# Attention products on 64x64 quarters, natural channel order, and moved q rows in a fused attention and feed-forward kernel

## The chip, the cores and the metric

The kernel runs on one core of a Trainium2 chip. A core has TensorE (PE, matrix products into PSUM), VectorE (DVE), ScalarE (ACT), GpSimd (POOL) and SyncE (SP); SP, POOL and ACT also start DMAs. The metric is the device time of one execution in microseconds (us). A profile of one execution gives every instruction's start and duration. On TensorE, "PEld" are the loads of the stationary operand and "PE" the matmuls, which are pipelined: a matmul's own duration is longer than the distance to the next one.

## What is computed

```python
q_s = exp(q - max(q, -1));  q_s /= sum(q_s, -1)        # softmax over the 64 channels of a head
k_s = exp(k - max(k, 2));   k_s /= sum(k_s, 2)         # softmax over the 576 rows of a head
kv  = einsum('bhsd,bhse->bhde', k_s, v)                # 64 x 64 for each head
x   = einsum('bhsd,bhde->bhse', q_s, kv)               # 576 x 64 for each head
x   = x.transpose(0, 2, 1, 3).reshape(4608, 512)       # row b*576+s, channel h*64+e
h   = x @ w_in                                         # 512 -> 2048
out = maximum(0.01 * h, h) @ w_out                     # 2048 -> 512
```

There are 8 batches, 8 heads, 576 rows and 64 channels a head, all in float32; the kernel multiplies in bfloat16.

## The kernel before

**Attention of one batch.** q, k and v lie in SBUF with 128 partitions: a partition holds nine rows of one head (`r`, 0 to 8), and one tile holds the eight heads as four pairs. A head's 576 rows are thus 64 partitions (`l`) by nine `r`. "Row r" below means these 64 rows of every head. Heads are counted as h = 4 gg + 2 hp + hh: hh is the upper or lower half of the partitions, gg and hp choose the pair. For k there are a maximum (`k_tree`, `k_allmax`), a subtraction (`k_sub`) and an exponential on ACT (`k_exp`); v is cast to bfloat16 with a column of ones beside it (`v_cast`). `kv_quads` (L318) multiplies exp(k) by v with 64x64 quarters of the array, 72 matmuls of 65 columns a batch, the last column being k's sum. `kd_make` (L338), or `kd_rec` and `kd_one` (L403, L407) in batch 0, divide by that sum and write `kd`: for each of four channel blocks g = 2 hh + gg a 128 x 128 matrix with the two heads hp = 0, 1 on its diagonal and zeros elsewhere (set once by POOL). q has a maximum (`q_max`), a subtraction on POOL (`q_sub`), an exponential on ACT (`q_exp`), a sum and reciprocal (`q_sum`) and a multiplication (`q_norm`) on VectorE, and a transpose. Batches 0 and 1 are transposed by TensorE (`q_transpose`) and copied out of PSUM (`q_keep`); later batches by a DMA that SP starts (`q_turn`). `attend` (L441) and `attend_x` (L468) then multiply `kd` by the transposed q, one full 128 x 128 matmul for each channel block and group of rows, and copy each product from PSUM into `xT`, which holds x transposed: 128 channels by 4608 rows in four blocks. Its channel blocks are in the order g = 2 hh + gg, so `load_w_in` (L130) permutes w_in's rows to match.

**Feed-forward.** The 4608 rows are nine tiles of 512. Layer 1 has 16 blocks j of 128 hidden channels, each four matmuls (channel blocks cb) into one PSUM bank, then `leaky` on ACT into `gj`. Layer 2 has four row blocks of 128 rows, 16 matmuls each, and VectorE copies the result out (`store`); SP writes it to memory. PSUM's eight banks are six of pool psB (layer 1, attention) and two of psO (layer 2).

**Order.** Every engine executes its instructions in the order of the code. `at(t, u, ...)` hangs attention work behind place u of tile t. In tiles 1 to 8 places 0 to 15 are the j of layer 1, and places 16 to 31 come after every four matmuls of layer 2 (19, 23, 27 and 31 end its row blocks); a place of 32 or more is one of the next tile. In tile 0 places 0 to 31 are the j of layer 1, first for rows 0 to 255 of the tile and then for rows 256 to 511, and 32 to 47 the j of layer 2, where all four row blocks take part in each j. Batch b is worked on in tiles b - 2 and b - 1 (`plan`), batch 2 in tile 1 (`plan2`), batches 0 and 1 ahead of and in tile 0. A batch has 576 rows and a tile 512, so tile 1 ends after row 6 of batch 1 and tile 2 after row 5 of batch 2.

**Loads.** SP loads q, k, v of batch 0, POOL starts w_in in eight pieces (four for hidden channels 0 to 1023, four for the rest). `hold_sync(0, ...)` (L599) makes SP wait for the first piece of the second half before it loads batch 1. POOL reads an element of the whole w_in (L607) before it starts five of w_out's six pieces. `hold_sync(1, ...)` (L610) makes SP wait for the piece of w_out with j = 8 to 11 before batch 2.

**Front of tile 0.** `begin` and `end` split layer 1's first half: blocks j = 0, 2, 4, 6 (two j a bank) take the channel blocks as products become ready, then j = 8 to 14, with pieces of batch 0's attention (x1, x3, t1, t2, x2) between.

Of the kernel before, what the change touches and what calls it, by code (L numbers as in the profile page):

```python
# [20 lines left out]
R = 9  # L21
# [4 lines left out]
def kernel(  # L26
# [99 lines left out]
    w_in_r = moe_w_in.rearrange("(gg hp hh d) f -> gg hp d hh f", gg=2, hp=2, hh=2)  # L126

    w_in_t = w_in_sb.rearrange("p (hh gg) f -> p gg hh f", gg=2)

    def load_w_in(fh):  # L130
        fs = slice(fh * (F // 2), (fh + 1) * (F // 2))
        for gg in range(2):
            for hp in range(2):
                nc.gpsimd.dma_start(  # L134
                    out=w_in_t[hp * D : (hp + 1) * D, gg, :, fs], in_=w_in_r[gg, hp, :, :, fs]
                )
# [201 lines left out]
    def kd_make(b):  # L338
        for hh in range(2):
            pkv = st[b]["pkv"][hh]  # L340
            krec = small_pool.tile([P, 2, 1], FP32, name="krec")
            nc.vector.reciprocal(out=krec, in_=pkv[:, :, D : D + 1])
            for hp in range(2):
                p0 = hp * D
                nc.vector.tensor_tensor(  # L345
                    out=kd2[b % 2][p0 : p0 + D, 2 * hh : 2 * hh + 2, p0 : p0 + D],
                    in0=pkv[p0 : p0 + D, :, 0:D],
                    in1=krec[p0 : p0 + D].to_broadcast([D, 2, D]),
                    op=ALU.mult,
                )  # L350

    wake_ps = psO_pool.tile([P, TT], FP32, name="pout")
# [54 lines left out]
    def kd_one(eng, b, gg, hh):  # L407
        pkv, krec = st[b]["pkv", gg][hh], st[b]["krec", gg, hh]
        eng.scalar_tensor_tensor(
            out=kd2[b % 2][:, 2 * hh + gg].rearrange("p (h d) -> p h d", h=2),  # L410
            in0=pkv[:, 0:D].unsqueeze(1).to_broadcast([P, 2, D]),
            scalar=krec,
            in1=block.rearrange("p (h d) -> p h d", h=2),
            op0=ALU.mult,
            op1=ALU.mult,
        )

    def q_transpose(b, r0, n):
        ps = psB_pool.tile([P, NB, n, L], BF16, name="psum_qt", tag=BANK_TAG)
# [21 lines left out]
    def attend(b, gs, c0, n, eng):  # L441

        ps = psB_pool.tile([P, len(gs), n], FP32, name="po", tag=BANK_TAG)
        for i, g in enumerate(gs):
            nc.tensor.matmul(
                ps[:, i],
                lhsT=kd2[b % 2][:, g],
                rhs=st[b]["qT"][:, g].rearrange("c r l -> c (r l)")[:, c0 : c0 + n],
                start=True,
                stop=True,  # L450
            )
        step = gs[-1] - gs[0] if len(gs) == 2 else 1
        o = xT[:, gs[0] : gs[-1] + 1 : step, b * S + c0 : b * S + c0 + n]
# [4 lines left out]


# [8 lines left out]
    def attend_x(b, g, rs, eng):  # L468
        hh, gg = divmod(g, 2)
        n = (rs.stop - rs.start) * L  # L470
        ps = psB_pool.tile([P, n], FP32, name="po", tag=BANK_TAG)
        qX = st[b]["qX"].rearrange("c (r g) (h l) -> c g h r l", g=2, h=2)
        nc.tensor.matmul(  # L473
            ps.rearrange("p (r l) -> p r l", l=L), lhsT=kd2[b % 2][:, g], rhs=qX[:, gg, hh, rs]
        )
        c0 = b * S + rs.start * L
        o = xT[:, g, c0 : c0 + n]
        if eng is nc.scalar:
            eng.copy(out=o, in_=ps)  # L479
        else:  # L480
            eng.tensor_copy(out=o, in_=ps)

    def layer1(j, ph, c0, n, part=slice(0, 4), first=True, last=True):
        for i, cb in list(enumerate((0, 2, 1, 3)))[part]:
# [4 lines left out]
                start=(i == 0 and first),  # L489
                stop=(i == NB - 1 and last),  # L490
# [36 lines left out]
    GS = (0, 2, 1, 3)  # L527
# [56 lines left out]
    attend(0, [0], 0, 256, nc.scalar)  # L584
    attend(0, [2], 0, 256, nc.scalar)
# [18 lines left out]
    def behind_first_units():  # L604
# [34 lines left out]
    def plan(b, o):  # L639
# [9 lines left out]
        kvu, pu = o + (24 if b == 3 else 25), o + (33 if b == 3 else 34)  # L649
# [3 lines left out]
        for i in range(8):  # L653
            at(t, pu + i // 2, lambda i=i: attend_x(b, i // 2, XR[i % 2], nc.scalar))


    def plan2():
# [13 lines left out]
        for i in range(8):  # L671
            at(1, 28 + i // 2, lambda i=i: attend_x(b, GS[i % 4], XR[i // 4], nc.scalar))
# [42 lines left out]
    for j, ph in zip(J0, begin(J0, ((0, x1), (1, x3)))):  # L715
        end(j, ph, 0, slice(2, 4), False)
# [72 lines left out]
```

## Time and profile before

| | us |
|---|---|
| median of 3 runs (lowest, highest) | 288.9 (288.86, 289.06) |
| the profiled execution: its time, its span | 288.9, 287.1 |
| before layer 1 of tile 0 | 0 to 15.0 |
| tile 0, layer 1 | 15.0 to 33.85 |
| tile 0, layer 2 | 33.85 to 51.38 |
| tiles 1, 2 | 29.52, 29.58 |
| tiles 3 to 6 | 29.45, 29.44, 29.42, 29.42 |
| tile 7 (no attention left) | 27.63 |
| tile 8 and the last stores | 31.26 |

Rows of a timeline give the start, the busy time, the engine, the line (L) of the kernel, the operation, output<-input, the shape and the number of instructions; in brackets stands the idle time before them and what ended it. TensorE's clock was granted in full (1.00) in all of these stretches.

### The profile page before, as it was taken

How to read it: one execution, taken by the hardware profiler on the slowest of the kernel's cores; microseconds unless marked ns; L12 is line 12 of the kernel's file. 1: busy time of each engine (PE TensorE's matmuls, PEld its weight loads, DVE VectorE, ACT ScalarE, POOL GpSimd, SP SyncE). 2: the span in 40 equal slices, each digit the busy share in tenths (PEclk: the TensorE clock that was granted, in tenths of full speed). 3: DMA queues.
4: the chain of work that ended last, by engine and by line, in shares of the span. 5: the costliest groups of instructions: out<-in, count | busy, mean ns of one | idle time of the engine just before them, and what ended most of it. 6: DMA issues, size and time to landing. Idle time of an engine off the chain costs nothing.

```text
span 287.1 us, 4854 instructions
## 1 busy us (share of the span) xinstructions
PE 275.8 (96%) x1927; PEld 136.4 (48%) x1954; DVE 145.7 (51%) x247; ACT 149.4 (52%) x272; POOL 89.6 (31%) x66
## 2 busy tenths in 40 slices
PE   8778999999999999999999999999999999999995
PEld 3357745444544444444444444444445444444443
DVE  3976946996880895398185727663631100110011
ACT  4965874567269407932774358434953065016400
POOL 4965550017049009604900590049100000000000
PEclk9999999999999999999999999999999999999999
DMA  7999999686659264963398239913131310130032
GB/s 257 317 210 354 288 181 404 170 274 258 134 109 378 106 142 104 398 159 82 76 379 195 56 82 351 237 37 80 32 84 37 73 37 3 45 81 20 2 73 73
DMA packets 36598, 45.79 MB, mean 159 GB/s; under 512 B 15968, under 2 KB 19296, under 8 KB 36576
## 3 DMA queue, kind: packets, MB, share of 16 engines
q1 hardware_dynamic: 33120, 41.16, 48.2%
q0 software_dynamic: 3296, 4.20, 8.3%
q8 instruction: 15, 0.25, 0.3%
q10 hardware_dynamic: 160, 0.13, 0.1%
q14 instruction: 7, 0.06, 0.1%
HBM read 36.70 MB, written 9.44 MB: 161 GB/s over the span
## 4 chain that ended last, share of the span: by engine, by line
PE 82%; DMA 10%; DVE 2%; POOL 1%; issue 1%; SPq 1%; ACT 1%; DVEq 0%; ACTq 0%
PE pout L506 39%; PE ph L485 38%; DMA v_raw<-in_v_dram 5%; DMA w_in_sb<-in_moe_w_in_dram 3%; PE po L473 2%; DMA k_raw<-in_k_dram 2%; PE pkv L323 2%; DVE qe L310 1%; DVE qsum L303 1%; SPq L79 1%; POOL w_in_sb L134 1%; POOL vb L216 0%; ACT qe L294 0%; PE psum_qt L422 0%; SPq L538 0%
## 5 line engine op out<-in xcount | busy, mean ns | idle before, releaser
L506 PE MATMUL pout<-w_out_sb,gj 128*128 128x512 bf16 (+2 forms) x580 | 129.5, 373 | 0.6
L485 PE MATMUL ph<-xT,w_in_sb 128*128 128x512 bf16 (+1 forms) x626 | 127.0, 357 | 3.0 <-DMA w_in_sb<-in_moe_w_in_dram 1.7
L494 ACT ACTIVATE gj<-ph 128x512 bf16<-128x512 f32 x144 | 81.8, 603 | 54.6 <-PE ph L485 54.0
L485 PEld LDWEIGHTS <-w_in_sb 128*128 128x128 bf16 x640 | 62.0, 98 | 64.1 <-issue 3.5
L506 PEld LDWEIGHTS <-gj 128*128 128x128 bf16 x592 | 56.8, 98 | 62.1 <-ACT gj L494 0.4
L500 DVE COPY out_sb<-pout 128x512 f32<-128x512 f32 (+1 forms) x34 | 22.7, 676 | 85.7 <-PE pout L506 80.0
L196 POOL TENSOR_TENSOR k_raw<-k_raw,kall 128x2304 f32<-128x2304 f32 (+1 forms) x6 | 29.1, 4856 | 80.1 <-DVE kall L188 67.5
L286 POOL TENSOR_TENSOR q_raw<-q_raw,qmax 128x2304 f32<-128x2304 f32 (+4 forms) x12 | 31.3, 2618 | 24.1 <-DVE qmax L227 23.7
L303 DVE TENSOR_REDUCE qsum<-qe 128x36 f32<-128x2304 bf16 (+4 forms) x12 | 19.9, 1661 | 36.4 <-ACT qe L294 36.4
L479 ACT CAST xT<-po 128x320 bf16<-128x320 f32 (+1 forms) x48 | 16.8, 402 | 40.0 <-PE po L473 40.0
L204 ACT ACTIVATE ke<-k_raw 128x2304 bf16<-128x2304 f32 (+2 forms) x11 | 17.6, 1597 | 10.5 <-POOL k_raw L196 9.0
L310 DVE TENSOR_TENSOR qe<-qe,qrec 128x2304 bf16<-128x2304 bf16 (+4 forms) x11 | 19.9, 1809 | 0.3
L227 DVE TENSOR_REDUCE qmax<-q_raw 128x36 f32<-128x2304 f32 (+4 forms) x12 | 19.6, 1649 | 0.0
L294 ACT ACTIVATE qe<-q_raw 128x2304 bf16<-128x2304 f32 (+4 forms) x12 | 17.0, 1420 | 0.0
L216 POOL CAST vb<-v_raw 128x1152 bf16<-128x1152 f32 x13 | 14.6, 1151 | 0.0
L163 DVE TENSOR_TENSOR t<-k_raw 128x1024 f32<-128x1024 f32 (+1 forms) x10 | 10.1, 1012 | 0.9 <-DMA k_raw<-in_k_dram 0.5
L163 DVE TENSOR_TENSOR t<-t 128x256 f32<-128x256 f32 (+2 forms) x20 | 9.6, 478 | 0.7
L473 PE MATMUL po<-qX,kd 128*128 128x320 bf16 (+1 forms) x48 | 9.8, 286 | 0.0
L500 ACT COPY out_sb<-pout 128x512 f32<-128x512 f32 (+1 forms) x3 | 1.7, 563 | 14.9 <-PE pout L506 14.9
L356 PE MATMUL pout<-zero 128*128 128x512 bf16 x23 | 7.5, 462 | 1.4 <-POOL zero L101 1.3
L345 DVE TENSOR_TENSOR kd<-pkv,krec 64x128 bf16<-64x128 f32 x28 | 8.1, 288 | 0.7
L323 PEld LDWEIGHTS <-ke 64*64 64x64 bf16 x576 | 5.6, 106 | 3.7 <-ACT gj L494 1.7
(62 smaller groups left out, 104.7 us busy)
## 6 DMA issues: line engine op xcount, KB each, us to landing
out_dram<-out_sb SPq DMA_DIRECT2D x70, 128.0 KB, 2.4
q_raw<-in_q_dram SPq DMA_DIRECT2D x7, 1152.0 KB, 8.0
v_raw<-in_v_dram SPq DMA_DIRECT2D x7, 1152.0 KB, 11.2
k_raw<-in_k_dram SPq DMA_DIRECT2D x6, 1152.0 KB, 5.5
k_raw<-in_k_dram SPq DMA_DIRECT2D x4, 576.0 KB, 5.5
w_in_sb<-in_moe_w_in_dram POOLq DMA_DIRECT2D x8, 256.0 KB, 7.5
v_raw<-in_v_dram SPq DMA_DIRECT2D x2, 576.0 KB, 7.1
w_out_sb<-in_moe_w_out_dram POOLq DMA_DIRECT2D x4, 256.0 KB, 9.7
```

The costliest lines, as they stand in the source:

```text
L163: nc.vector.tensor_tensor(out=o, in0=i0, in1=i1, op=ALU.max)
L196: eng.tensor_tensor(out=ks, in0=ks, in1=st[b]["kall"][:, hs].unsqueeze(2).to_broadcast([P, n, R, D]), op=ALU.subtract,)
L204: nc.scalar.activation(out=st[b]["ke"][:, :, hs].rearrange("p r h d -> p h r d"), in_=st[b]["k"][:, hs], func=AF.Exp,)
L227: nc.vector.tensor_reduce(out=m, in_=st[b]["q"][:, :, rs], axis=AX.X, op=ALU.max)
L286: eng.tensor_tensor(out=qs, in0=qs, in1=st[b]["qmax", rs.start].unsqueeze(3).to_broadcast([P, HL, n, D]), op=ALU.subtract,)
L294: nc.scalar.activation(out=st[b]["qe"][:, rs].rearrange("p r h d -> p h r d"), in_=st[b]["q"][:, :, rs], func=AF.Exp,)
L303: nc.vector.reduce_sum(out=qsum, in_=st[b]["qe"][:, rs], axis=AX.X)
L310: eng.tensor_tensor(out=qes, in0=qes, in1=st[b]["qrec", rs.start].unsqueeze(3).to_broadcast([P, n, HL, D]), op=ALU.mult,)
L485: nc.tensor.matmul(ph, lhsT=w_in_sb[:, cb, j * P : (j + 1) * P], rhs=xT[:, cb, c0 : c0 + n], start=(i == 0 and first), stop=(i == NB - 1 a ...
L494: nc.scalar.activation(out=o, in_=ph, func=AF.Prelu, alpha=LEAKY_SLOPE)
L500: copy(out=out_sb, in_=pout)
L506: nc.tensor.matmul(pout, lhsT=g_sb[j // 2][:, j % 2, tsub * P : (tsub + 1) * P], rhs=w_out_sb[:, j, os], start=(j == 0), stop=(j == NF - 1),)
```

## The change

- `kd` holds for each head its 64 x 64 matrix alone, without zeros. `cross` multiplies it by that head's transposed q on one 64x64 quarter: rows of the quarter by hp, columns by hh, so four heads (one gg) go to four quarters, with the outputs of hp = 0 and hp = 1 in two banks. Channel blocks of `xT` are then 2 gg + hp, the natural order of channels, and w_in is loaded in natural order, one piece for each channel block and half.
- A batch's products stand at one place of the code (`attend_all`): all quarters first, then the copies out of PSUM. For batches 3 to 7 that is place 27 (b < 5) or 23 of tile b - 1, for rows 0 to 7 and row 8; before, they stood in four pairs at four places between 19 and 31. Batch 2: rows 0 to 5 at place 27 of tile 1, rows 6 to 8 at place 19 of tile 2.
- Batch 1: rows 0 to 6 in tile 0. Rows 7 and 8 (RE): maximum at place 31, subtraction and exponential at 32 and 44 of tile 0, sum and norm at place 12 of tile 1, transposes at 15, products at 23. One of v's two casts goes from ACT to POOL, and the exponential of rows 0 to 3 moves ahead of the other cast.
- Batch 0: the front of tile 0 is rewritten. Each group of blocks takes cb 0, 1, 2 in `begin` and cb 3 in `end_pe`; `leaky` comes in `end_act`. The second half no longer starts between the pieces of the first. The norm of rows 4 and 5 goes from POOL to VectorE, two transposes use psO.

```diff
-    block = const_pool.tile([P, P], FP32)
-    nc.gpsimd.memset(block, 0.0)
-    for p0 in range(0, P, D):
-        nc.gpsimd.memset(block[p0 : p0 + D, p0 : p0 + D], 1.0)
...
-    kd2 = [const_pool.tile([P, NB, P], BF16, name=f"kd{i}") for i in range(2)]
+    kd2 = [const_pool.tile([P, 2, 2, D], BF16, name=f"kd{i}") for i in range(2)]
...
-        nc.gpsimd.memset(kd2[i], 0.0)
...
+        for cb in range(NB):
+            nc.gpsimd.dma_start(out=w_in_sb[:, cb, fs], in_=w_in_r[:, cb, fs])
...
-            for hp in range(2):
-                p0 = hp * D
-                nc.vector.tensor_tensor(
-                    out=kd2[b % 2][p0 : p0 + D, 2 * hh : 2 * hh + 2, p0 : p0 + D],
...
+            nc.vector.tensor_tensor(
+                out=kd2[b % 2][:, :, hh],
+                in0=pkv[:, :, 0:D],
+                in1=krec.to_broadcast([P, 2, D]),
+                op=ALU.mult,
+            )
...
+        eng.tensor_tensor(
+            out=kd2[b % 2][:, gg, hh], in0=pkv[:, 0:D], in1=krec.to_broadcast([P, D]), op=ALU.mult
+        )
...
+    def cross(b, gg, outs, rows):
+        for hp in range(2):
+            for hh in range(2):
+                half = slice(hp * D, (hp + 1) * D)
+                if "qX" in st[b]:
+                    rhs = st[b]["qX"].rearrange("c (r g) (h l) -> c g h r l", g=2, h=2)[:, gg, hh, rows]
+                else:
+                    rhs = st[b]["qT"][:, 2 * hh + gg, rows]
+                nc.tensor.matmul(
+                    outs[hp][hh * D : (hh + 1) * D].rearrange("p (r l) -> p r l", l=L),
+                    lhsT=kd2[b % 2][half, gg, hh],
+                    rhs=rhs[half],
+                    start=True,
+                    stop=True,
+                )
+
+    def attend(b, ggs, rows):
+        n = (rows.stop - rows.start) * L
+        ps = [
+            psB_pool.tile([P, len(ggs), n], FP32, name="po", tag=BANK_TAG) for _ in range(2)
+        ]
+        for i, gg in enumerate(ggs):
+            cross(b, gg, [ps[hp][:, i] for hp in range(2)], rows)
+        st[b]["po", ggs, rows.start] = ps
+
+    def x_keep(eng, b, ggs, rows, hp):
+        ps = st[b]["po", ggs, rows.start][hp]
...
+        o = xT[:, s0 : 2 * ggs[-1] + hp + 1 : 2, c0:c1]
...
+    def attend_rows(b, rows, engs=(nc.scalar, nc.scalar)):
+        groups = ((0, 1),) if rows.stop - rows.start <= 4 else ((0,), (1,))
+        for ggs in groups:
+            attend(b, ggs, rows)
+        return [
+            lambda ggs=ggs, hp=hp: x_keep(engs[hp], b, ggs, rows, hp) for ggs in groups for hp in range(2)
+        ]
+
+    def attend_all(b, *parts):
+        for fn in sum([attend_rows(b, *p) for p in parts], []):
+            fn()
...
-    at(0, 0, lambda: q_sum(0, R1), lambda: q_norm(0, R1, nc.gpsimd), behind_first_units)
-    at(0, 2, lambda: q_exp(0, R2), lambda: q_sum(0, R2), lambda: q_norm(0, R2))
...
-    at(0, 26, lambda: attend(0, [0, 1, 2, 3], 512, 64, nc.scalar))
+    at(0, 26, lambda: attend_all(0, (R3, (nc.scalar, nc.vector))))
...
+    RM, RE = slice(4, 7), slice(7, R)
+    for rs in (RA, RM):
+        at(0, 20, lambda rs=rs: q_max(1, rs), lambda rs=rs: q_sub(nc.gpsimd, 1, rs))
+    at(0, 31, lambda: k_exp(1, H1), lambda: k_exp(1, H0), lambda: q_max(1, RE))
...
-    at(0, 32, lambda: v_cast(nc.scalar, 1, 1), lambda: q_exp(1, RB), lambda: q_sum(1, RB))
-    at(0, 41, lambda: kv(1))
-    at(0, 41, lambda: q_norm(1, RB), lambda: kd_make(1))
+    at(0, 32, lambda: v_cast(nc.scalar, 1, 0), lambda: v_cast(nc.gpsimd, 1, 1))
+    at(0, 32, lambda: q_exp(1, RM), lambda: q_sum(1, RM), lambda: q_norm(1, RM))
+    at(0, 32, lambda: q_sub(nc.gpsimd, 1, RE))
     for r0 in (0, 2):
...
+        at(0, 42, lambda r0=r0: q_transpose(1, r0, 2), lambda r0=r0: q_keep(nc.scalar, 1, r0, 2))
+    at(0, 42, lambda: kv(1), lambda: kd_make(1))
+    at(0, 44, lambda: q_transpose(1, 4, 3), lambda: q_keep(nc.scalar, 1, 4, 3), lambda: q_exp(1, RE))
+    at(0, 46, lambda: attend_all(1, (slice(0, 7), (nc.scalar, nc.vector))))
+    at(1, 12, lambda: q_sum(1, RE), lambda: q_norm(1, RE))
+    at(1, 15, lambda: q_transpose(1, 7, 2), lambda: q_keep(nc.scalar, 1, 7, 2))
+    at(1, 23, lambda: attend_all(1, (RE,)))
+
+    XR = (slice(0, 6), slice(6, R))
...
-        for i in range(8):
-            at(t, pu + i // 2, lambda i=i: attend_x(b, i // 2, XR[i % 2], nc.scalar))
+        at(b - 1, 27 if b < 5 else 23, lambda: attend_all(b, (slice(0, 8),), (slice(8, R),)))
...
+        at(1, 27, lambda: attend_all(b, (XR[0],)))
+        at(2, 19, lambda: attend_all(b, (XR[1],)))
...
+    def end_act(j, ph, half):
+        leaky(g_sb[j // 2][:, :, 256 * half : 256 * half + 256], ph)
+        for h in range(2):
             run(0, 16 * half + j + h)
 
-    t1 = (lambda: q_transpose(0, 4, 2), lambda: q_keep(nc.scalar, 0, 4, 2), lambda: q_exp(0, R3))
-    t2 = (lambda: q_transpose(0, 6, 2), lambda: q_keep(nc.vector, 0, 6, 2), lambda: q_sum(0, R3))
+    t2 = (
+        lambda: q_transpose(0, 6, 2, psO_pool, "pout"),
+        lambda: q_keep(nc.vector, 0, 6, 2),
+        lambda: q_sum(0, R3),
+    )
     x2 = (
-        lambda: attend(0, [0, 2], 256, 256, nc.scalar),
-        lambda: attend(0, [1, 3], 256, 256, nc.vector),
+        lambda: attend_all(0, (slice(4, 8), (nc.scalar, nc.vector))),
         lambda: q_norm(0, R3),
     )
-    x1 = (lambda: attend(0, [1], 0, 256, nc.scalar),)
-    x3 = (lambda: q_exp(0, R1), lambda: attend(0, [3], 0, 256, nc.scalar))
-
-    def whole(j):
-        end(j, psB_pool.tile([P, 2, 256], FP32, name="ph", tag=BANK_TAG), 1, slice(0, 4), True)
+    x1 = (
+        lambda: attend(0, (1,), RA),
+        lambda: x_keep(nc.scalar, 0, (1,), RA, 0),
+        lambda: q_exp(0, R1),
+        lambda: x_keep(nc.scalar, 0, (1,), RA, 1),
+    )
 
...
+    begun = list(zip(J0, begin(J0, ((0, x1), (1, ()), (2, ())))))
+    for j, ph in begun:
+        end_pe(j, ph, 0, slice(3, 4), False)
+    for i, (j, ph) in enumerate(begun):
+        end_act(j, ph, 0)
+        if i == 0:
+            q_sum(0, R1)
+            q_norm(0, R1)
+            q_exp(0, R2)
+            late_loads()
+            q_sum(0, R2)
+            q_norm(0, R2)
+        if i == 1:
+            q_transpose(0, 4, 2, psO_pool, "pout")
+            q_keep(nc.scalar, 0, 4, 2)
+    q_exp(0, R3)
+    for j, ph in zip(J1, begin(J1, ((0, t2), (1, x2), (2, ())))):
+        end_pe(j, ph, 0, slice(3, 4), False)
+        end_act(j, ph, 0)
+    for j in range(0, NF, 2):
+        ph = psB_pool.tile([P, 2, 256], FP32, name="ph", tag=BANK_TAG)
+        end_pe(j, ph, 1, slice(0, 4), True)
+        end_act(j, ph, 1)
```

More of the change, by code (lines that the diff above doesn't have):

```diff
@@ L439, in q_keep @@
             eng.tensor_copy(out=o, in_=i)
[L441 to L453, printed above, removed]
+    def cross(b, gg, outs, rows):
[23 more added lines that the diff above has]
+        ps = st[b]["po", ggs, rows.start][hp]
+        c0, c1 = b * S + rows.start * L, b * S + rows.stop * L
+        s0 = 2 * ggs[0] + hp
+        o = xT[:, s0 : 2 * ggs[-1] + hp + 1 : 2, c0:c1]
         if eng is nc.scalar:
@@ L466, in q_turn @@
         )
[L468 to L481, printed above, removed]
     def layer1(j, ph, c0, n, part=slice(0, 4), first=True, last=True):
-        for i, cb in list(enumerate((0, 2, 1, 3)))[part]:
+        for cb in range(NB)[part]:
             nc.tensor.matmul(
@@ L488, in layer1 @@
                 rhs=xT[:, cb, c0 : c0 + n],
-                start=(i == 0 and first),
-                stop=(i == NB - 1 and last),
+                start=(cb == 0 and first),
+                stop=(cb == NB - 1 and last),
             )
@@ L526 @@
     H0, H1 = slice(0, 2), slice(2, 4)
-    GS = (0, 2, 1, 3)
     def load_all(b):
@@ L722 @@
-    for j in range(4, NF, 2):
-        whole(j)
-    pout = [psO_pool.tile([P, O], FP32, name="pout") for _ in range(2)]
+    x1 = (
[4 more added lines that the diff above has]
+    )
+    J0, J1 = range(0, 8, 2), range(8, NF, 2)
+    begun = list(zip(J0, begin(J0, ((0, x1), (1, ()), (2, ())))))
[13 more added lines that the diff above has]
+            q_keep(nc.scalar, 0, 4, 2)
@@ L725 @@
+    q_exp(0, R3)
[6 more added lines that the diff above has]
+        end_act(j, ph, 1)
+    pout = [psO_pool.tile([P, O], FP32, name="pout", tag="pout") for _ in range(2)]
     pout += [psB_pool.tile([P, O], FP32, name="pout2", tag=BANK_TAG) for _ in range(2)]
```

58 lines of the change are left out of this document (11 added, 47 removed).

## The prediction

> **What bounds the kernel now.** I read the page's busy times and chain first, then TensorE's timeline over the whole span, then the other engines' timelines from 11 to 82 us, and last the busy times by tile.
>
> ```profile
> PE 275.8 (96%) x1927; PEld 136.4 (48%) x1954; DVE 145.7 (51%) x247; ACT 149.4 (52%) x272; POOL 89.6 (31%) x66
> PE 82%; DMA 10%; DVE 2%; POOL 1%; issue 1%; SPq 1%; ACT 1%; DVEq 0%; ACTq 0%
> ```
>
> TensorE sets the end; the 18% of the chain that is not TensorE is nearly all in the first 51 us. So the edit has two prices: its TensorE time in the steady tiles, and its waits around tile 0. One steady tile in TensorE's timeline, then two pieces of a tile with no attention in it:
>
> ```profile
> 139.93 9.66 PE L485 MATMUL ph<-xT,w_in_sb 128*128 128x512 bf16 x43
> 149.52 0.80 PE L323 MATMUL pkv<-vb,ke 64*64 64x65 bf16 x72
> 150.25 4.49 PE L485 MATMUL ph<-xT,w_in_sb 128*128 128x512 bf16 x19
> 154.58 3.62 PE L506 MATMUL pout<-w_out_sb,gj 128*128 128x512 bf16 x16
> 158.03 0.41 PE L473 MATMUL po<-qX,kd 128*128 128x320 bf16 x2
> 158.28 1.03 PE L506 MATMUL pout<-w_out_sb,gj 128*128 128x512 bf16 x4
> ...
> 161.60 7.93 PE L506 MATMUL pout<-w_out_sb,gj 128*128 128x512 bf16 x36
> ...
> 228.21 13.98 PE L485 MATMUL ph<-xT,w_in_sb 128*128 128x512 bf16 x62
> 242.03 13.98 PE L506 MATMUL pout<-w_out_sb,gj 128*128 128x512 bf16 x63
> ```
>
> 64 matmuls of 512 columns take 242.03 - 228.21 = 13.82, so 0.216 each (0.42 ns a column). A tile without attention is 27.63. Eight attention matmuls cost 161.60 - 158.03 less twelve 512-column ones, 3.57 - 2.59 = 0.98 us a batch. The 72 kv matmuls already run on 64x64 quarters: layer 1 with them takes 154.58 - 139.93 = 14.65, so 0.83. They are 18 rounds of four with 65 columns; four at once need 18 x 0.027 = 0.49, so 0.34 is switching and per-round loss. Single starts in the trace split it: 0.09 before the first, 0.12 after the last, 7 ns a round.
>
> Tile 0 on the DMA queue of SP and on TensorE:
>
> ```profile
> 19.82 0.63 SPq L538 DMA_DIRECT2D held<-w_in_sb  x1
> 40.02 0.52 SPq L538 DMA_DIRECT2D held<-w_out_sb  x1
> 20.85 1.03 PE L485 MATMUL ph<-xT,w_in_sb 128*128 128x256 bf16 x8 [1.39 <-DMA w_in_sb<-in_moe_w_in_dram]
> 33.85 8.80 PE L506 MATMUL pout<-w_out_sb,gj 128*128 128x512 bf16 x39
> 46.97 0.72 PE L422 MATMUL psum_qt<-ident,qe 128*128 128x128 bf16 x10 [0.44 <-DVE kd L345]
> 51.38 13.97 PE L485 MATMUL ph<-xT,w_in_sb 128*128 128x512 bf16 x62
> ```
>
> SP's two rows wait for a load: the fifth piece of w_in landed at 19.8, rows 8 to 11 of w_out at 40.0. Layer 2 of tile 0 starts at 33.85 and reaches j = 8 eight times 0.864 later, at 40.76: 0.7 us after its weights.
>
> **The change, part by part.**
>
> *Quarters in the steady tiles.* A batch of nine rows becomes two rounds of 512 columns and two of 64: 0.43 + 0.05, plus 0.21 of switching and 4 x 7 ns: 0.72 against 0.98, a gain of 0.26. Bounds for the switch: 0.21 (kv's two gaps) to 0.34 (all its loss), so 0.26 to 0.13; I take the first, since its parts were read singly. Batches 3 to 7: **-1.3** (bounds -1.3 to -0.65). Batch 2, split 6 and 3: 0.32 + 0.24 in tile 1; its rows 6 to 8 stand in tile 2 right ahead of kv(3), in the same mode, so 0.17 without a switch.
>
> *Evictions.* Six a batch for eight, all ACT's: four of 512 (0.59 us; six such in a row on ACT took 3.22, 0.54 apart) and two of 128 (0.3 by the 64-to-256 rows): 2.8. They now follow one stretch. At place 23 two row blocks (6.9 us) cover them, at 27 one (3.46): hidden. The last pair in tile 2 now made layer 1 wait (that tile takes 29.58 against 29.42): **-0.14**.
>
> *kd, memsets, w_in.* kd_make loses two of four multiplies, kd_one its mask: 0.1 to 0.6 us on VectorE per batch, which waits for TensorE there; five memsets leave POOL at 2.2 to 4.2, where it then waited for k until 7.5. Nothing. w_in goes in the same eight pieces of 256 KB at the same places in POOL's queue, so I keep the landings: 13.6, 14.9, 16.2, 17.4, then 19.8, 20.7, 22.0, 23.2 (landing times in the trace; SP's row, TensorE's at 20.85 and POOL's read of w_in at 23.35 agree).
>
> *Front of tile 0.* With kd ready by 15.9, layer 1 for the first half goes 15.0 (cb 0), 15.9 quarters (0.32), 16.2 (cb 1), 17.1 (cb 2), 18.0 (cb 3), 18.8 end. Before, it ended at 19.45. The q chain: exp of rows 4, 5 on ACT 16.6 to 17.2, sum and norm on VectorE to 18.9, transposes then; rows 6, 7 by the same steps at 21.0. j = 8 to 15 is then paced by w_in: 19.95, 21.3 after the transposes, 22.6 after the quarters, last block from 23.45, end 24.3. Second half: 64 x 0.1095 = 7.0 plus 0.4 for row 8: layer 2 starts near **31.8**, 2.1 earlier. But w_out's DMAs stand in POOL's queue behind the read of the whole w_in, as before, and SP's loads of batch 1 behind the same 19.8. So j = 8 still waits for 40.0: it starts at 40.15, 0.6 earlier and no more. 0.85 us of the front may go wrong at no cost.
>
> *Batch 1 in tile 0.* From 40.15: eight j (6.91), 14 transposes at 0.055 (0.77), kv 0.83, quarters for seven rows 0.37 + 0.22. The 0.44 wait goes: on ACT the exp of rows 0 to 3 no longer stands behind the cast of v (landed at 37.9), ends at 38.8, and VectorE norms them by 41.6 (TensorE wants them at 42.7), rows 4 to 6 by 43.7 (wanted at 45.8). The cast on POOL ends near 40.3. The evictions, two on ACT, two on VectorE, have 0.86 us of j = 15 ahead of layer 1, whose cb 3 comes 0.65 later: enough, so the 0.46 wait at 50.92 goes too. Tile 1 starts at **49.25**, that is **-2.1**; if that last wait stays, -1.6.
>
> *Rows 7, 8 of batch 1 in tile 1.* Place 12 puts sum, reciprocal and norm (0.69 + 0.20 + 0.69, with gaps 1.64) on VectorE behind the q maxima of batch 2, and place 15 has TensorE transpose the result right behind layer 1. What VectorE does before it:
>
> ```profile
> 51.79 2.47 DVE L500 COPY out_sb<-pout 128x512 f32<-128x512 f32 x4
> ...
> 62.11 2.60 DVE L227 TENSOR_REDUCE qmax<-q_raw 128x20 f32<-128x1280 f32 x2
> 67.49 1.49 DVE L303 TENSOR_REDUCE qsum<-qe 128x20 f32<-128x1280 bf16 x1 [2.77 <-ACT qe L294]
> ```
>
> From the stores to the end of the maxima VectorE is busy 62.11 + 2.60 - 51.79 = 12.92 with no wait. The stores will start at 49.45, so the norm ends at 49.45 + 12.92 + 1.64 = 64.0; TensorE is through layer 1 at 49.25 + 13.82 = 63.07. **A new wait of 0.95**, behind which the whole of layer 2 stands. Bounds: 0.7 if the small gaps between VectorE's instructions close, 1.2 if the stores start 0.41 behind layer 1 as they do now. Then four transposes 0.24, quarters 0.12 (shared with kv(2)). Behind it, norm of batch 2's rows 0 to 5 ends near 70.3, its DMA transpose lands 3 to 5 us later (before: issued 71.54, last piece at 76.48), TensorE wants it at 75.5: hidden, by little.
>
> **Sum**, against the profiled run's own 288.9 (span 287.1 and 1.8 around it; the median of three is 288.9 too): tile 0 -2.1; tile 1 +0.95 + 0.24 + 0.12 and -0.98 + 0.56 for batch 2; tile 2 +0.17 - 0.14; batches 3 to 7 -1.3. Together -2.5: **286.4**.
>
> **Rivals.**
>
> *The late rows cost nothing.* Were VectorE a microsecond ahead, the 0.95 would go: 285.4. For it: VectorE has 2.77 idle at 64.7. Against: that idle lies behind the maxima, where it helps nothing.
>
> *The late rows cost twice.* VectorE's delay passes to the DMA transpose, and place 27 of tile 1 waits too: 0.2 there (issue 70.45, 4.94 as before, 0.3 for the sixth row: 75.7 against 75.5), 0.4 more if the norm of six rows is slowed as the one of five was (2.06 against 1.49 the time before), and 0.25 at place 15 with the wait at its upper bound: 287.25. For it: the last piece landed 0.85 ahead of its use before. Against: fifteen of its sixteen pieces landed two us sooner.
>
> *Evictions become the bound.* Six products now finish in 0.7 us. If ACT took each at its full row plus a wait (0.8 and 0.5: 4.2), the 3.7 us behind places 27 would leave 0.5 in three tiles: 287.8. Against: the 0.54 spacing. The Trainium skill says this too (TensorEngine Tiling (Array Packing), "PSUM Bottleneck": tiling speeds up TensorE but not the eviction, which may become the bottleneck); by it the sum would be this rival's, and no row before shows six evictions behind one stretch.
>
> *Slower: the quarters run two at a time.* kv's rounds of four stream only 65 columns. If two quarters that read the same 64 partitions took turns over 512 columns, each round would double: +0.48 a batch over seven batches, 3.4 in all: 289.8. It decides from 1.7 times the single round on (2.5 us over 7 x 1,152 columns of 0.42 ns). Against: kv's rounds start 0.03 apart, which two turns of 0.027 don't fit.
>
> *Nothing comes of tile 0*: another load or norm holds layer 2 to its old times, 288.5.
>
> **How the numbers follow.** Forecast 0.55; late rows free 0.10; late rows twice 0.12; evictions 0.06; tile 0 without gain 0.07; quarters by twos, or another slowdown of that size, 0.10. The likeliest gives 286.4, with its own range 285.6 to 287.2. The low end of the range is the free rows with a somewhat better tile 0, 285.0; the high end takes in evictions and most of tile 0's failure, 288.5. This kernel can tell about 0.2%, 0.6 us: faster 0.81, same 0.07, slower 0.12.
>
> **What would show it.** Attention matmuls as 64x64 rows of four per round, 0.7 us between the neighbours; a TensorE wait for w_out near 40; layer 1 of tile 1 from 49.3; a TensorE wait of about 1 us on VectorE's norm near 63; steady tiles of 29.15 for 29.42. Wrong: a steady tile over 29.42, layer 1 waiting on ACT's copies, or tile 1 starting after 50.5.

## The result

| | before | after |
|---|---|---|
| median of 5 runs (lowest, highest), us | 288.88 (288.70, 289.06) | 287.44 (287.28, 288.14) |
| the profiled execution: its time, its span | 288.9, 287.1 | 287.5, 285.7 |

The ratio is 0.9954, with a 95% interval of 0.994 to 0.9969: faster by 1.4 us, where 2.5 were forecast. The shares of the chain that ended last, on the page after:

```profile
PE 79%; DMA 10%; DVE 5%; POOL 3%; issue 1%; SPq 0%; DVEq 0%; POOLq 0%
```

TensorE's share of the chain fell from 82% to 79% and VectorE's rose from 2% to 5%: that points at VectorE, and the timelines show where. TensorE's timeline after, from the end of layer 1 of tile 0:

```profile
31.91 5.34 PE L502 MATMUL pout<-w_out_sb,gj 128*128 128x512 bf16 x24
37.49 1.89 PE L502 MATMUL pout<-w_out_sb,gj 128*128 128x512 bf16 x8 [0.25 <-DMA w_out_sb<-in_moe_w_out_dram]
40.34 2.75 PE L502 MATMUL pout<-w_out_sb,gj 128*128 128x512 bf16 x12 [0.95 <-DMA w_out_sb<-in_moe_w_out_dram]
...
49.47 13.98 PE L481 MATMUL ph<-xT,w_in_sb 128*128 128x512 bf16 x64
65.07 0.40 PE L405 MATMUL psum_qt<-ident,qe 128*128 128x128 bf16 x4 [1.62 <-DVE qe L300]
...
73.21 3.63 PE L502 MATMUL pout<-w_out_sb,gj 128*128 128x512 bf16 x16
76.77 0.52 PE L432 MATMUL po<-qX,kd 64*64 64x384 bf16 x8
...
80.68 13.98 PE L481 MATMUL ph<-xT,w_in_sb 128*128 128x512 bf16 x64
...
153.93 7.07 PE L502 MATMUL pout<-w_out_sb,gj 128*128 128x512 bf16 x32
160.93 0.69 PE L432 MATMUL po<-qX,kd 64*64 64x512 bf16 x16
161.55 7.08 PE L502 MATMUL pout<-w_out_sb,gj 128*128 128x512 bf16 x32
```

Layer 2 of tile 0 starts 1.94 earlier and waits for w_out at j = 6 (37.49) and at j = 8 (40.34). Tile 1 begins at 49.47. At 65.07 stands the new wait, the four transposes of rows 7 and 8 of batch 1, and it is 1.62 long. In the steady tile the sixteen quarters of a batch cost 161.55 - 160.93 = 0.62 from their first start to the next matmul. The gap ahead of them adds 0.09 (153.93 and 32 times 0.216 give 160.84): 0.71 between their neighbours, where 0.72 was forecast. By stage, a tile counted from its first matmul to that of the next:

| us | before | forecast | after | after less forecast |
|---|---|---|---|---|
| tile 1 starts | 51.38 | 49.25 | 49.47 | +0.22 |
| tile 1 | 29.52 | 30.41 | 31.21 | +0.80 |
| tile 2 | 29.58 | 29.35 | 29.41 | +0.06 |
| tiles 3 to 6, sum | 117.73 | 116.69 | 116.70 | 0.01 |
| tile 7 | 27.63 | 27.63 | 27.63 | 0 |
| tile 8 and the last stores | 31.26 | 31.26 | 31.28 | +0.02 |

The forecast column is each step of the prediction added to before. The last column adds up to 1.11, the whole miss of the profiled execution, and 0.80 of it lies in tile 1.

VectorE in tile 1, then GpSimd's instruction that ran beside it:

```profile
59.83 2.61 DVE L217 TENSOR_REDUCE qmax<-q_raw 128x24 f32<-128x1536 f32 x2
62.35 0.68 DVE L293 TENSOR_REDUCE qsum<-qe 128x8 f32<-128x512 bf16 x1
63.06 0.20 DVE L295 RECIPROCAL qrec<-qsum 128x8 f32<-128x8 f32 x1
63.30 1.72 DVE L300 TENSOR_TENSOR qe<-qe,qrec 128x512 bf16<-128x512 bf16 x1
```

```profile
61.71 2.76 POOL L276 TENSOR_TENSOR q_raw<-q_raw,qmax 128x1536 f32<-128x1536 f32 x1 [20.08 <-DVE qmax L217]
```

The norm of rows 7 and 8 (63.30) took 1.72 where the prediction put 0.69. A sum, reciprocal and norm of the prediction's durations (0.69, 0.20, 0.69) stand near 20 us of the kernel before, and GpSimd did nothing beside that norm; VectorE, then GpSimd's next instruction:

```profile
20.29 0.69 DVE L310 TENSOR_TENSOR qe<-qe,qrec 128x512 bf16<-128x512 bf16 x1
```

```profile
23.35 0.18 POOL L607 CAST gate<-w_in_sb 128x1 f32<-128x1 bf16 x1 [3.48 <-DMA w_in_sb<-in_moe_w_in_dram]
```

After the change GpSimd's subtraction of batch 2 starts when the first of VectorE's maxima is there and runs until 64.47; the norm ends at 65.02, 0.55 behind it. The sum at 62.35, also inside the subtraction, took its usual 0.68.

### The profile page after: what moved, and what is told of

The parts are those of the page before. It is cut to its first block, busy times and chain, and to the rows that moved or that the text cites. A ratio compares the mean times of both kernels' runs of the same rounds, so it can differ in the third digit from the quotient of the medians.

```text
span 285.7 us, 4988 instructions
## 1 busy us (share of the span) xinstructions
PE 275.9 (97%) x2022; PEld 132.8 (46%) x2022; DVE 142.4 (50%) x237; ACT 146.1 (51%) x260; POOL 88.4 (31%) x62
## 4 chain that ended last, share of the span: by engine, by line
PE 79%; DMA 10%; DVE 5%; POOL 3%; issue 1%; SPq 0%; DVEq 0%; POOLq 0%
PE pout L502 41%; PE ph L481 34%; DMA w_out_sb<-in_moe_w_out_dram 5%; DMA w_in_sb<-in_moe_w_in_dram 3%; DMA k_raw<-in_k_dram 2%; PE pkv L313 2%; PE po L432 2%; POOL w_in_sb L126 1%; DVE out_sb L496 1%; DVE qmax L217 1%; DVE t L153 1%; POOL w_out_sb L131 1%; DVE qe L300 1%; DVE k_raw L186 0%; PE psum_qt L405 0%
## 5 line engine op out<-in xcount | busy, mean ns | idle before, releaser
L502 PE MATMUL pout<-w_out_sb,gj 128*128 128x512 bf16 (+2 forms) x592 | 128.1, 373 | 1.2 <-DMA w_out_sb<-in_moe_w_out_dram 1.2
L455 ACT CAST xT<-po 128x512 bf16<-128x512 f32 (+4 forms) x46 | 18.3, 483 | 46.0 <-PE po L432 46.0
L276 POOL TENSOR_TENSOR q_raw<-q_raw,qmax 128x2304 f32<-128x2304 f32 (+5 forms) x13 | 32.0, 2464 | 22.1 <-DVE qmax L217 21.4
L293 DVE TENSOR_REDUCE qsum<-qe 128x36 f32<-128x2304 bf16 (+5 forms) x13 | 20.1, 1544 | 32.9 <-ACT qe L284 32.9
L300 DVE TENSOR_TENSOR qe<-qe,qrec 128x2304 bf16<-128x2304 bf16 (+5 forms) x13 | 22.2, 1705 | 0.4
L217 DVE TENSOR_REDUCE qmax<-q_raw 128x36 f32<-128x2304 f32 (+5 forms) x13 | 19.8, 1537 | 0.0
L284 ACT ACTIVATE qe<-q_raw 128x2304 bf16<-128x2304 f32 (+5 forms) x13 | 17.2, 1326 | 1.2 <-POOL q_raw L276 1.2
L206 POOL CAST vb<-v_raw 128x1152 bf16<-128x1152 f32 x14 | 15.7, 1150 | 0.0
L313 PE MATMUL pkv<-vb,ke 64*64 64x65 bf16 x576 | 6.8, 194 | 0.2
L231 ACT ACTIVATE qe<-q_raw,nmax 128x64 bf16<-128x64 f32 x16 | 5.3, 333 | 3.2 <-DVE nmax L226 3.2
```

Source lines behind the costliest of these rows:

```text
L217: nc.vector.tensor_reduce(out=m, in_=st[b]["q"][:, :, rs], axis=AX.X, op=ALU.max)
L276: eng.tensor_tensor(out=qs, in0=qs, in1=st[b]["qmax", rs.start].unsqueeze(3).to_broadcast([P, HL, n, D]), op=ALU.subtract,)
L293: nc.vector.reduce_sum(out=qsum, in_=st[b]["qe"][:, rs], axis=AX.X)
L300: eng.tensor_tensor(out=qes, in0=qes, in1=st[b]["qrec", rs.start].unsqueeze(3).to_broadcast([P, n, HL, D]), op=ALU.mult,)
L313: nc.tensor.matmul(outs[hh][hp * D : (hp + 1) * D, 0 : D + 1], lhsT=st[b]["ke"][rows, r, 2 * gg + hp], rhs=vb2[b % 2][rows, r, gg, hp, 0 : ...
L502: nc.tensor.matmul(pout, lhsT=g_sb[j // 2][:, j % 2, tsub * P : (tsub + 1) * P], rhs=w_out_sb[:, j, os], start=(j == 0), stop=(j == NF - 1),)
```

## The experiments

**Theory.** The norm has two operands in SBUF and was held until GpSimd's subtraction was over; that is the missing microsecond. **Rivals.** The wait is in the place of the transposes and passes on if they move; the norm is long for another reason; or switching the array or the copies out of PSUM cost more than was taken. Before, run beside these, had medians of 288.85 to 289.17.

### The transposes later

```diff
-    at(1, 15, lambda: q_transpose(1, 7, 2), lambda: q_keep(nc.scalar, 1, 7, 2))
+    at(1, 19, lambda: q_transpose(1, 7, 2), lambda: q_keep(nc.scalar, 1, 7, 2))
```

> Only the place of batch 1's last transposes (rows 7 and 8) and their copy changes, from 15 to 19 of tile 1; VectorE's order stays. Theory (TensorE's 1.62 us wait at place 15 is the missing gain): place 19 is reached about 3.5 us later, at 66.8, when the norm (end 65.0) is done, so no TensorE wait is left there; layer 2 then reaches j = 14 near 66.3 and waits about 0.3 for the last two leaky on ACT (end 66.5 and 67.0 in the changed kernel). Gain 1.4, time 286.0. Rival (the wait only passes on to the DMA transpose of batch 2, wanted at place 27): a new wait of 0.5 to 1.0 at place 27, time 286.5 to 287.0.

Measured: 286.07 us (285.96 to 286.17), ratio 0.9893 [0.9879, 0.9907]. TensorE's timeline:

```profile
49.21 13.98 PE L481 MATMUL ph<-xT,w_in_sb 128*128 128x512 bf16 x63
63.03 4.12 PE L502 MATMUL pout<-w_out_sb,gj 128*128 128x512 bf16 x15
66.99 0.39 PE L405 MATMUL psum_qt<-ident,qe 128*128 128x128 bf16 x4
...
75.22 0.52 PE L432 MATMUL po<-qX,kd 64*64 64x384 bf16 x8
...
79.13 13.98 PE L481 MATMUL ph<-xT,w_in_sb 128*128 128x512 bf16 x62
```

The norm still takes 1.72 (63.04 in VectorE's timeline), but nobody waits for it now, and place 27 (75.22) follows without a wait: the delay does not pass on. Tile 1 takes 79.13 - 49.21 = 29.92 for 31.21, so that moving the wait away gave 1.29 us, nearly as much as the change had gained (1.44). It is not the whole wait: the first row block now takes 66.99 - 63.03 = 3.96, which is 0.50 more than its sixteen matmuls, where 0.3 was expected for the last two leaky. The time fell by 1.37, because tile 1 also starts earlier in this execution (49.21 for 49.47): w_out lands at times that differ between executions. SP's row that waits for it starts between 40.05 and 40.45 in the changed kernel and the six runs that leave these loads alone.

### The norm earlier, while GpSimd is idle

```diff
+    at(0, 42, lambda: q_exp(1, RE))
...
+    at(0, 44, lambda: q_sum(1, RE), lambda: q_norm(1, RE))
...
-    at(1, 12, lambda: q_sum(1, RE), lambda: q_norm(1, RE))
```

The exponential is taken away from its old place behind the copy at place 44.

> The exponential of rows 7 and 8 of batch 1 goes to place 42 of tile 0 (ACT is idle from 41.0 to 43.4), their sum and norm to place 44 (VectorE is idle from 45.6 to 48.6); the transposes stay at place 15. Theory: no wait at place 15, and about 0.3 behind ACT's last leaky; time 286.0, as with the transposes moved. Theory on the long norm (1.72 us against 0.69 for the same shape in the kernel before): it was held while POOL subtracted q's maximum, so here, with POOL idle, the row shows 0.69. Rival: the norm is long because of its own operands or place, and takes 1.7 here too; then VectorE's copies out of PSUM come 0.8 late and tile 1 starts later than 49.5.

Measured: 285.8 us (285.79 to 285.96), ratio 0.9886 [0.9869, 0.9902]. The row in VectorE's timeline, GpSimd's instructions before and after it, and TensorE's tile 1:

```profile
46.21 0.69 DVE L300 TENSOR_TENSOR qe<-qe,qrec 128x512 bf16<-128x512 bf16 x1
```

```profile
40.30 1.03 POOL L276 TENSOR_TENSOR q_raw<-q_raw,qmax 128x512 f32<-128x512 f32 x1
61.52 4.19 POOL L276 TENSOR_TENSOR q_raw<-q_raw,qmax 128x1536 f32<-128x1536 f32 x2 [20.19 <-DVE qmax L217]
```

```profile
49.28 13.98 PE L481 MATMUL ph<-xT,w_in_sb 128*128 128x512 bf16 x63
...
78.98 13.98 PE L481 MATMUL ph<-xT,w_in_sb 128*128 128x512 bf16 x62
```

The same instruction takes 0.69 with GpSimd idle (41.3 to 61.5). And GpSimd's two subtractions of batch 2, with no norm beside them, take 4.19 for 4.64 after: the hold goes both ways. Tile 1 takes 78.98 - 49.28 = 29.70 for 31.21.

### GpSimd made to wait

The run above moves the norm. This one leaves it in its place on VectorE, behind the two maxima, and moves GpSimd's work behind it.

```diff
-    at(1, 12, lambda: q_sum(1, RE), lambda: q_norm(1, RE))
...
-            at(1, 9, lambda rs=rs: q_max(b, rs), lambda rs=rs: q_sub(nc.gpsimd, b, rs))
+            at(1, 9, lambda rs=rs: q_max(b, rs))
+        at(1, 12, lambda: q_sum(1, RE), lambda: q_norm(1, RE))
+        at(1, 12, lambda: nc.gpsimd.tensor_copy(out=gate[:, 0:1], in_=st[1]["qe"][:, R - 1, HL - 1, D - 1 : D]))
+        for rs in XR:
+            at(1, 12, lambda rs=rs: q_sub(nc.gpsimd, b, rs))
```

> GpSimd's two subtractions of batch 2 are put behind a read of the normed rows 7 and 8, so that GpSimd has nothing to do while VectorE norms them. Theory (a product of two SBUF operands on VectorE is held for as long as a GpSimd instruction runs): the norm of rows 7 and 8 takes 0.69 us again instead of 1.72, ends near 64.0, and TensorE's wait at place 15 of tile 1 is 0.7 to 0.8 us instead of 1.62. The subtraction then starts about 2.4 us later than now, which makes the exponential of batch 2's rows late; ScalarE does it ahead of leaky of blocks 14 and 15, so layer 2 of tile 1 waits near j = 14 for about 1.7: the time does not get better by it, about 288.3. Rival (something else makes the norm long, such as the two q maxima just ahead of it or its place in the code): it takes 1.7 with GpSimd idle.

Measured: 288.67 us (one run). VectorE, then TensorE:

```profile
59.97 2.61 DVE L217 TENSOR_REDUCE qmax<-q_raw 128x24 f32<-128x1536 f32 x2
...
63.44 0.69 DVE L300 TENSOR_TENSOR qe<-qe,qrec 128x512 bf16<-128x512 bf16 x1
```

```profile
49.60 13.98 PE L481 MATMUL ph<-xT,w_in_sb 128*128 128x512 bf16 x63
64.19 0.40 PE L405 MATMUL psum_qt<-ident,qe 128*128 128x128 bf16 x4 [0.61 <-ACT gj L490]
...
69.22 4.33 PE L502 MATMUL pout<-w_out_sb,gj 128*128 128x512 bf16 x18 [1.61 <-ACT gj L490]
```

At its old place, behind the same two maxima, the norm takes 0.69 and ends at 64.13, 0.06 before the transposes start. (The profile names ScalarE for the 0.61, whose last leaky before it ends at 64.15. But the transposes follow the norm as closely as in the changed kernel, where they start at 65.07 behind 65.02 and that leaky had ended a microsecond earlier. So it was the norm that released them.) The transposes are late by 64.19 - (49.60 + 13.82) = 0.77, inside the bounds of the prediction. The rival that something else makes the norm long is out. The price came at j = 14, as expected: ScalarE's exponential of batch 2 is late and leaky behind it.

### A longer front

Eight matmuls of 256 columns more ahead of layer 1's second half; their result is overwritten, the output is the same.

```diff
+        if j == 0:
+            for _ in range(2):
+                layer1(0, ph[:, 0], 256, 256)
```

> Eight matmuls of 256 columns more (0.88 us) ahead of layer 1's second half in tile 0; their result is overwritten, the output stays. Theory (layer 2 of tile 0 waits for w_out at j = 8, so the front has 0.95 us to spare): layer 2 starts at 32.8 for 31.9, the wait at j = 8 falls from 0.95 to about 0.1, tile 1 still starts near 49.5, time 287.4 unchanged within 0.2. Rival (the front sets tile 0's end): time 288.3.

Measured: 287.57 us (287.34 to 287.95), ratio 0.9947 [0.993, 0.9963].

```profile
33.01 9.94 PE L502 MATMUL pout<-w_out_sb,gj 128*128 128x512 bf16 x43
...
49.33 2.97 PE L481 MATMUL ph<-xT,w_in_sb 128*128 128x512 bf16 x13
```

Layer 2 of tile 0 starts 1.1 later, and tile 1 starts no later: w_out's landing, not the front, sets tile 0's end. The first row runs over a wait too short to be marked: j = 8 would start at 33.01 + 8 times 0.864 = 39.92, and a narrower window of the same timeline has it at 40.19. So 0.27 of the wait for w_out is left (0.1 was expected), and even this front sets nothing.

### w_out's fifth piece in two

```diff
-        for j0, j1 in ((2, 4), (4, 6), (6, 8), (8, 12), (12, 16)):
+        for j0, j1 in ((2, 4), (4, 6), (6, 8), (8, 10), (10, 12), (12, 16)):
```

> The piece of w_out for j = 8 to 11 is loaded as two pieces (8, 9 and 10, 11) at the same place. Theory A (the wait at j = 8 is worth its 0.95 us): j = 8 starts near 39.3, tile 1 at 48.6, time 286.5. Theory B (VectorE's norm of rows 0 to 3 of batch 1, which ended at 42.72 while TensorE wanted it at 42.9, is right behind): TensorE waits 0.6 to 0.7 at place 42 in its stead, tile 1 starts at 49.2, time 287.2. I hold B for likelier.

Measured: 287.03 us (286.97 to 287.52), ratio 0.993 [0.9916, 0.9943]. TensorE, then VectorE:

```profile
37.94 4.48 PE L502 MATMUL pout<-w_out_sb,gj 128*128 128x512 bf16 x20 [0.40 <-DMA w_out_sb<-in_moe_w_out_dram]
42.45 0.61 PE L405 MATMUL psum_qt<-ident,qe 128*128 128x128 bf16 x8
...
48.99 3.19 PE L481 MATMUL ph<-xT,w_in_sb 128*128 128x512 bf16 x14
```

```profile
40.36 1.94 DVE L300 TENSOR_TENSOR qe<-qe,qrec 128x1024 bf16<-128x1024 bf16 x1
```

The wait for j = 8 is gone, one of 0.40 for j = 6 is left. The transposes at place 42 start 0.15 behind the norm of rows 0 to 3 (40.36 + 1.94 = 42.30) and 0.19 behind the place that the twenty matmuls leave them (37.94 + 20 times 0.216 = 42.26). So that norm is the next limit, as theory B said, but by 0.19 and not by 0.6; it too is longer than before the change (1.23).

### Three stretches instead of one

```diff
+        if b < 5:
+            at(b - 1, 27, lambda: attend_all(b, (slice(0, 8),), (slice(8, R),)))
+        else:
+            at(b - 1, 21, lambda: attend_all(b, (slice(0, 4),)))
+            at(b - 1, 22, lambda: attend_all(b, (slice(4, 8),)))
+            at(b - 1, 23, lambda: attend_all(b, (slice(8, R),)))
```

> The products of batches 5, 6 and 7 stand in three stretches (rows 0 to 3, 4 to 7, row 8, at places 21, 22 and 23) instead of one; the matmuls are the same, but TensorE goes to 64x64 quarters and back three times instead of once. By the prediction's price of a switch pair, 0.21, tiles 4 to 6 take 29.6 for 29.18, and the time is about 288.7; by its upper bound of 0.34 they take 29.86. Rival (switching costs nothing measurable, the gain came from the four-fold rounds alone): 29.2 and the time of the changed kernel.

Measured: 288.99 us (one run). TensorE at the start of tiles 4 and 5:

```profile
139.32 9.66 PE L481 MATMUL ph<-xT,w_in_sb 128*128 128x512 bf16 x43
...
168.97 9.66 PE L481 MATMUL ph<-xT,w_in_sb 128*128 128x512 bf16 x44
```

Tiles 4 to 6 take 29.65, 29.63 and 29.64 for 29.19, 29.16 and 29.16. The expectation that the matmuls are the same does not quite hold: rows 0 to 7 come in four rounds of 256 columns instead of two of 512, which at the prediction's 7 ns a round is about 0.01. Two more pairs of switches thus cost about 0.47, 0.23 a pair, near the lower of the prediction's bounds (0.21 to 0.34). Switching does cost: with three stretches the tile (29.64) is longer than before the change (29.42), so the gain needs the one stretch.

### The products without cover

```diff
-        at(b - 1, 27 if b < 5 else 23, lambda: attend_all(b, (slice(0, 8),), (slice(8, R),)))
+        at(b - 1, 31, lambda: attend_all(b, (slice(0, 8),), (slice(8, R),)))
```

> The products of batches 3 to 7 stand at place 31, behind the last row block of a tile instead of one or two blocks ahead of it, so that nothing covers their copies out of PSUM. The first copy ends about 1.1 us after the stretch starts and they follow each other 0.54 apart, while layer 1 of the next tile wants the last channel block 0.65 after its start: if the copies' rate is what the prediction took (0.54), layer 1 waits about 1.5 us in each of five tiles, the steady tile is 30.7 for 29.18, and the time is near 294.9. If each copy took 0.8 (the prediction's rival on evictions), about 2.8 a tile. Rival (the copies are never on the path): no change.

Measured: 293.93 us (one run). ScalarE's copies, and TensorE around them:

```profile
140.46 2.39 ACT L455 CAST xT<-po 128x512 bf16<-128x512 f32 x6 [0.42 <-PE po L432]
```

```profile
140.01 0.69 PE L432 MATMUL po<-qX,kd 64*64 64x512 bf16 x16
141.09 10.48 PE L481 MATMUL ph<-xT,w_in_sb 128*128 128x512 bf16 x43 [0.39 <-ACT xT L455]
...
170.47 0.69 PE L432 MATMUL po<-qX,kd 64*64 64x512 bf16 x16
```

The tile takes 170.47 - 140.01 = 30.46 for 29.18: 1.28, of which 0.39 stands as a wait and most of the rest lies inside layer 1, whose first row takes 10.48 for the 9.66 of the steady tile. Six copies are done in 2.4 us, less than the 2.8 forecast. Where the change put them, 3.5 or 6.9 us of layer 2 cover that.

### Both gains together, and two steps on

The earlier norm and the split piece in one kernel:

> Rows 7 and 8 of batch 1 are summed and normed in tile 0, while GpSimd has nothing to do, and w_out's rows 8 to 11 come in two pieces. Theory: the two gains are at different places and add up: tile 1 starts near 48.95, layer 1 and layer 2 follow each other without a wait at place 15, tile 1 takes 29.7, and the time is about 285.5. Rival (the earlier sum and norm delay VectorE's copies at the end of tile 0, which the earlier weights make tighter): a wait at layer 1 of tile 1, and 285.8 or more.

Measured: 285.52 us (285.35 to 285.67), ratio 0.9875 [0.9859, 0.9892]. VectorE, GpSimd, then TensorE:

```profile
40.44 1.94 DVE L300 TENSOR_TENSOR qe<-qe,qrec 128x1024 bf16<-128x1024 bf16 x1
```

```profile
40.26 1.04 POOL L276 TENSOR_TENSOR q_raw<-q_raw,qmax 128x512 f32<-128x512 f32 x1
```

```profile
42.52 0.61 PE L405 MATMUL psum_qt<-ident,qe 128*128 128x128 bf16 x8 [0.42 <-DVE qe L300]
...
49.07 13.98 PE L481 MATMUL ph<-xT,w_in_sb 128*128 128x512 bf16 x63
62.88 0.39 PE L405 MATMUL psum_qt<-ident,qe 128*128 128x128 bf16 x4
```

As expected, and at place 42 TensorE now waits for the norm of rows 0 to 3, held (1.94) while GpSimd subtracts rows 7 and 8. Two edits on top of it were tried. Both give v's second cast to ScalarE; the first also starts w_out's pieces earlier:

```diff
-        nc.gpsimd.tensor_copy(out=gate[:, 0:1], in_=w_in_sb[:, NB - 1, F - 1 : F])
+        nc.gpsimd.tensor_copy(out=gate[:, 0:1], in_=w_in_sb[:, 1, F - 1 : F])
...
-    at(0, 32, lambda: v_cast(nc.scalar, 1, 0), lambda: v_cast(nc.gpsimd, 1, 1))
+    at(0, 32, lambda: v_cast(nc.scalar, 1, 0), lambda: v_cast(nc.scalar, 1, 1))
```

> As the run with both gains (rows 7 and 8 summed and normed in tile 0, rows 8 to 11 of w_out in two pieces), and in addition the second cast of batch 1's v moves from GpSimd to ScalarE, and GpSimd starts w_out's pieces behind the second of w_in's second-half pieces instead of the whole of w_in. Theory: with GpSimd idle, or with only its subtraction, the norm of rows 0 to 3 takes 1.23 as it did before the change, instead of 1.94, and the transposes at place 42 wait for nothing; the weights for j = 6 and 8 land about 1 us earlier, so that tile 1 starts near 48.6 and the time is about 285.1. Rival (the loads share one memory path: w_out's earlier pieces make batch 1's q and v, or w_in's last pieces, later by as much): the wait is at w_in in layer 1's second half or at the norm, tile 1 starts at 49.1 or later, 285.5 or more.

Measured: 286.07 us (285.83 to 286.16), ratio 0.9903 [0.9887, 0.992]. No wait for w_out is marked any more, but batch 1's loads, started at the same times within 0.1, land later: q takes 14.2 us from issue to landing instead of 11.7, v 19.4 instead of 17.0. VectorE, then TensorE:

```profile
41.35 1.22 DVE L300 TENSOR_TENSOR qe<-qe,qrec 128x1024 bf16<-128x1024 bf16 x1
```

```profile
42.72 0.61 PE L405 MATMUL psum_qt<-ident,qe 128*128 128x128 bf16 x8 [0.92 <-ACT vb L204]
```

The norm of rows 0 to 3 is not held any more (1.22), but it starts 0.91 later and ends at 42.57, and the transposes follow 0.15 behind it, as in the run with the split piece (0.15) and the run with both gains (0.14). The profile names v's cast, which ends at 42.61; the transposes read the norm's result and nothing of v. So the rival was right in time and place, the wait is at the norm. Its reason, loads that share one path, fits: w_out started earlier and batch 1's loads landed later. What they share was not tested further. The second edit alone:

> As the run with both gains, with one edit: the second cast of batch 1's v goes to ScalarE, as the first, and w_out's pieces stay where they are. GpSimd's subtraction of rows 7 and 8 then runs at 39.2 to 40.3 and is over before VectorE norms rows 0 to 3 at 40.4. Theory: that norm takes 1.22 instead of 1.94 and ends near 41.7, the transposes at place 42 of tile 0 follow layer 2's matmuls at 42.1 with no wait, tile 1 starts near 48.65, and the time is about 285.1. Rival (the cast, on ScalarE now, makes the exponential of rows 4 to 6 or the kv products late): a wait at place 42 or 44 as long as the one it takes away, 285.5 or more.

Measured: 285.28 us (284.93 to 285.43), ratio 0.987 [0.9853, 0.9886]. VectorE, GpSimd, then TensorE:

```profile
40.57 1.23 DVE L300 TENSOR_TENSOR qe<-qe,qrec 128x1024 bf16<-128x1024 bf16 x1
```

```profile
36.01 4.33 POOL L276 TENSOR_TENSOR q_raw<-q_raw,qmax 128x1024 f32<-128x1024 f32 x3
```

```profile
37.99 4.48 PE L502 MATMUL pout<-w_out_sb,gj 128*128 128x512 bf16 x20 [0.54 <-DMA w_out_sb<-in_moe_w_out_dram]
42.31 0.61 PE L405 MATMUL psum_qt<-ident,qe 128*128 128x128 bf16 x8
...
48.86 13.98 PE L481 MATMUL ph<-xT,w_in_sb 128*128 128x512 bf16 x63
```

With GpSimd's subtraction over at 40.3, the norm takes 1.23 instead of 1.94, a second place where the theory holds. Tile 1 starts at 48.86, not the 48.65 expected, because w_out landed later in this execution (TensorE waits 0.54 for it, 0.18 in the run with both gains). Its interval overlaps with the one of the two gains alone, so only the profile says that the step helped. Both of these, 285.52 and 285.28, beat the changed kernel and the one before.

## Why the prediction was right, and where it was off

The sign and the steps were right: 287.44 lies in the range given (285.0 to 288.5), but 0.24 above the likeliest case's own (285.6 to 287.2).

- *Quarters in the steady tiles*: forecast 0.26 a batch, measured 29.42 - 29.16 = 0.26. The run with three stretches puts the price of a switch near its lower end; quarters by twos are out, since sixteen of them cost 0.71 with both gaps, where twos would have made it 1.20.
- *Evictions*: hidden, as forecast. The Trainium skill (TensorEngine Tiling (Array Packing), "PSUM Bottleneck") says that the copies may become the bottleneck once tiling speeds TensorE up. With the products at place 31, where nothing covers the copies, the trace agrees (1.28 a tile); at the change's places no row shows it.
- *Tile 0*: -1.91 for -2.1. Layer 2's start (31.91 for 31.8), the wait for w_out and the end of the waits of 0.44 and 0.46 came as told; j = 8 started 0.19 later than forecast, and that went through to tile 1. It is within the 0.4 by which w_out's landing differs between executions. The extra matmuls show that the front's slack was real. One more step here was off at no cost: the norm of rows 0 to 3 ended at 42.72, not 41.6, held by GpSimd's subtraction, and TensorE came for it at 42.92. That it did not show is luck; the runs with earlier weights paid for it.
- *Rows 7, 8 of batch 1 in tile 1* is the step that failed, in size and not in kind: the wait at place 15 was put at 0.95, with bounds of 0.7 and 1.2. On the same count, from layer 1's start plus 13.82, it was 65.07 - 63.29 = 1.78. The term that was mis-sized is the norm, 1.72 for 0.69: its row (20.29) came from a stretch in which GpSimd was idle. The rest of that sum held as a whole: with 0.69 the norm would have ended at 63.30 + 0.69 = 63.99, and 64.0 was forecast. (The stores started 0.17 later than forecast and VectorE's work behind them closed up by as much.) The wait is 0.83 too long and not 1.03, because layer 1 ended 0.22 later than forecast. GpSimd's subtraction waits for the very maxima that stand ahead of the norm on VectorE, so the two were bound to meet. The prediction had seen such a pair before (2.06, beside GpSimd's casts of v, against 1.49) and applied it only to batch 2's norm, in a rival.
- *The late rows cost twice* named 287.25, nearest to the result, by another mechanism: place 27 waits for nothing after the change (76.77). That a number fits is no proof of its story.
- *The late rows cost nothing*, 285.4: made true by moving the norm or the transposes, it gives 285.8 and 286.07.

The Trainium skill states the missing rule (SBUF — State Buffer, "Who interferes with whom"): a VectorE instruction with two inputs in SBUF and a GpSimd instruction that reads SBUF exclude each other for the whole of an instruction, and a tensor_reduce is never held. The trace agrees: 1.72 against 0.69, 1.94 against 1.23, and 0.68 for the sum beside GpSimd's subtraction.

## What to carry to other kernels

Before a duration is taken from a row, look at what the other engines do where the instruction will stand: an elementwise product of two SBUF tensors on VectorE beside a GpSimd instruction such as the subtractions here is to be priced to that instruction's end and nearly its own time on top, and GpSimd's next one as longer by what the product then takes. Of a wait that layer 2 of a tile stands behind, 1.3 to 1.5 of 1.6 us came back here; moving its consumer by four groups of four matmuls was worth nearly as much as the whole rearrangement. When a load is made earlier, ask which load lands later for it. Where the profile names one engine for a wait on several, compare the distances to each of them with a run in which only one could be the cause.

## What was not expected of the hardware

The hold goes both ways and is not shared out. GpSimd's first subtraction (2.76) was not slowed, and the norm ended 0.55 behind its end, less than its 0.69 alone; the second subtraction then took 1.92 instead of 1.47, and the pair 4.64 instead of 4.19. With rows 0 to 3, VectorE's 1.23 became 1.94 beside a subtraction of 1.04. Why a held norm ends a little sooner after the release than it takes alone was not settled.
